# Fourier mixing and a gated feed-forward: batch 1's input in one run, and a transpose cut in four pieces

## The chip, the cores and the metric

The kernel runs on one core of a Trainium2 chip. The metric is the device time of one execution in microseconds (us). The engines are named as in the profile: PE is TensorE, DVE is VectorE, ACT is ScalarE, POOL is GpSimd and SP is SyncE, which only issues transfers.

## What is computed

```python
# x: (8, 3008, 256); filters: (1505, 256) real and imaginary; feed-forward 256 -> 1536 -> 256
X = np.fft.rfft(x, axis=1)
Y = X * (filt_r + 1j * filt_i)[None]
y = np.fft.irfft(Y, n=3008, axis=1).reshape(24064, 256)
out = (np.maximum(y @ w_gate, 0) * (y @ w_val)) @ w_out
```

## The kernel before

A sequence of 3008 = 94 x 32 rows is transformed in two steps, and back in two. Step A is a transform of length 94 by matmul, step B one of length 32, then the filter's product, then the two inverse steps. The order of all instructions is written out by hand: each engine does its own in the order of the program, and semaphores hold it until its inputs are there and its outputs may be overwritten.

Batches 0 and 1 take step A from x in fp32, loaded into XF0 and XF1 (`load_x`, L185; 16 columns of 256 each, 96 partitions in three transfers). `first_a(b, p, s, h, copy)` (L278) is one sixteenth of step A for batch b: `p` picks a quarter of the 32 columns (p = 0 and 1 lie in XF0, p = 2 and 3 in XF1), `s` a half of that quarter and `h` one half of the 256 channels. A matmul goes to a bank of PSUM, and ACT copies it as bf16 into the tile `AS[b][h]`. `turn_a(b, h)` (L288) then transposes one half, 128 x 2048 as fp32 words, in blocks of 32 x 32 on DVE into `at`, which step B reads.

`first_b` (L419) is step B, the product and the first inverse step of batch 0, in six groups `i`: `fwd` (PE, into psX), `product` (DVE, or ACT and POOL, into tt and uu), and `inv` (L389: PE into psD, a copy to `dsb`, and every one or two groups a store to `Dbuf` in device memory, L416). The store that ends with group 3 is issued by ACT, the others by SP. After each group `amid(i)` puts in other work: spare matmuls (`warm`), the rest of batch 1's x after group 3, half of the gate and value weights after group 5 (`load_vg`, POOL), and one `first_a` of batch 1 after each of groups 4 and 5 and after the last but one `inv`. The last store of D, two copies wide, comes out of the tile `AS[0][0]`.

`load_d(b, z0, z1, engs)` (L438) reads D back in four chunks `z`, two transfers of 48 partitions each. Chunk 0 of batch 0 is read by SP and ACT, chunk 1 by SP, chunks 2 and 3 by POOL behind the second half of the weights. `hold_gpsimd` makes POOL wait for chunk 0. `item_c(k, h)` (L459) is the last inverse step for block k of 512 rows: PE into psY, and a copy to yT (half 0 by ACT, half 1 by DVE). The 13 `first_a` of batch 1 that are left, and its two `turn_a`, stand around the first `item_c`.

The feed-forward runs over 47 blocks of 12 steps. `gv` (L476) is a step: four matmuls into psV and psG, ACT's copy `vsb`, and DVE's `prod`; `o_part` adds four matmuls for the block before. Other work is bound to a step by `at_step`: clearing of the chunks XP (POOL) at step 2, the other batches' step A on POOL and PE, step B of batch 1 from step 16 on, and `item_c` of the next block at steps 8 and 10 of each block. PSUM's eight banks are taken in turn, so a step can't be more than four steps ahead of its `prod`.

The tiles of the start (XF, AS, tabs, tt, uu, xs) lie in a pool `pro` that is closed ahead of the feed-forward, whose pool `fs` (vsb, prod, XP and others) takes its place. In the program as built, the first `vsb` waits for the transpose of `AS[1][1]`.

Of the kernel before, what the change touches and what calls it, by code (L numbers as in the profile page):

```python
# [12 lines left out]
FP32 = mybir.dt.float32  # L13
BF16 = mybir.dt.bfloat16
# [15 lines left out]
N1, N2 = 94, 32  # L30
NROW = 96
NG = 24
# [3 lines left out]
def _ap(t, offset_elems, ap_list):  # L36
    return dataclasses.replace(
        t, offset=t.offset + offset_elems, ap=[list(p) for p in ap_list]
    )
# [81 lines left out]
def kernel(  # L121
# [10 lines left out]
    nc = tc.nc  # L132
    B, S_, D = x.shape
# [3 lines left out]
    NC2 = 8  # L137
# [11 lines left out]
    sb = ctx.enter_context(tc.tile_pool(name="sb", bufs=2))  # L149
# [3 lines left out]
    def bank(name, *shape):  # L153

        i = free.pop(0)
        t = ps.tile([128, *shape], FP32, tag=f"bank{i}", bufs=1, name=name)
        held[id(t)] = i, t
        return t

    def done(t):  # L160
        free.append(held.pop(id(t))[0])

    prologue = ExitStack()
    pro = prologue.enter_context(tc.tile_pool(name="pro", bufs=1))

    Abuf = [dram.tile([NROW * N2, D], BF16, name=f"Abuf{b}") if b > 1 else None for b in range(B)]
    Dbuf = [dram.tile([NROW * N2, D], BF16, name=f"Dbuf{b}") for b in range(B)]

    XF = [pro.tile([128, NX2 * D], FP32, name=f"XF{c}") for c in range(N2 // NX2)]
    WA = pro.tile([128, 128], FP32)  # L170
    AS = [[pro.tile([128, NC2, N2 // NC2, D // 2], BF16, name=f"AS{b}{h}") for h in range(2)]
          for b in range(2)]
    WF = consts.tile([128, 4, 32], FP32)
    M1 = consts.tile([NROW, N1], BF16)
    F2 = consts.tile([128, NG, 64], BF16)
# [9 lines left out]
    def load_x(b, engs, cols, ms=range(3)):  # L185
        w = NX2 * D
        for c, c0, c1 in cols:
            for m in ms:
                rows = min(32, B * N1 - (b * N1 + 32 * m))
                engs[m % len(engs)].dma_start(XF[c][m:m + 4 * rows - 3:4, c0:c1],  # L190
                              _ap(x, (b * N1 + 32 * m) * N2 * D + c * w + c0,
                                  [[N2 * D, rows], [1, c1 - c0]]))
# [57 lines left out]
    def place_filter(fi, a, half, copy):  # L250

        dst = FILT[fi][1]
        gs = slice(H * half, H * half + H)
        r = a * 64
        copy(dst[r + 32:r + 64, gs, :], dst[r:r + 32, gs, :])

    def place_nyq():
        for (src, dst), n in zip(FILT, nyq):
            nc.gpsimd.tensor_copy(dst[96:97, NG - 1, :], n)

    def load_vg(c0, c1):
        for (w_hbm, w_sb) in ((moe_w_val, WvT), (moe_w_gate, WgT)):
            nc.gpsimd.dma_start(w_sb[:, :, c0:c1],
                                _ap(w_hbm, c0, [[DFF, 128], [128 * DFF, 2], [1, c1 - c0]]))
# [7 lines left out]
    def hold_gpsimd(tile_):  # L272

        scr = sb.tile([128, 8], FP32, tag="scr", bufs=2)
        nc.gpsimd.tensor_copy(scr[:tile_.shape[0]], tile_)  # L275


    def first_a(b, p, s, h, copy):  # L278

        psA = bank("psA", 4, D // 2)  # L280
        xf = XF[p // 2].rearrange("p (n d) -> p n d", d=D)
        n = p % 2 * NC2 + 4 * s
        nc.tensor.matmul(psA, WA, xf[:, n:n + 4, h * D // 2:(h + 1) * D // 2],  # L283
                         start=True, stop=True)
        copy(AS[b][h][:, 4 * s:4 * s + 4, p, :], psA)
        done(psA)

    def turn_a(b, h):  # L288

        if h == 0:  # L290
            ats[b] = sb.tile([128, 32, D], BF16, tag="at", bufs=1, name="at")
        src = AS[b][h].rearrange("p l c d -> p (l c) d").bitcast(FP32).rearrange("p n d -> p d n")
        dst = ats[b].bitcast(FP32).rearrange("p k d -> p d k")
        nc.vector.transpose(dst[:, h * D // 4:(h + 1) * D // 4, :], src)  # L294

    fold = {}

# [91 lines left out]
    def inv(b, i, cuts=CUTS):  # L389

        if i in cuts:
            if (b, i) == (0, 5):
                dsb = AS[0][0].rearrange("p (a o) c d -> p a (o c d)", a=2)
                dsb = dsb.rearrange("p a (o d) -> p a o d", d=D)
            else:
                dsb = sb.tile([128, 2, 4, D], BF16, tag="dsb", bufs=3, name="dsb")
            dsbs[b] = i, dsb
        i0, dsb = dsbs[b]
        psD = [bank("psD", 2, D) for a in range(2)]
        for m in range(2):  # L400
            for k in range(2):
                for a in range(2):
                    for e in range(2):
                        nc.tensor.matmul(psD[a][64 * e:64 * e + 64, m],  # L404
                                         (I2t, I2u)[k][64 * a:64 * a + 64, 4 * i + 2 * m + e, :],
                                         tus[b, i, e, k][64 * a:64 * a + 64, m],
                                         start=(k == 0), stop=(k == 1),
                                         tile_position=(64 * a, 64 * e))
        o = 2 * (i - i0)
        for a in range(2):  # L410
            copy = nc.vector.tensor_copy if (b, i, a) == (0, 5, 0) else nc.scalar.copy
            copy(dsb[:, a, o:o + 2, :], psD[a])  # L412
            done(psD[a])
        if i + 1 in cuts:
            eng = nc.scalar if (b, i) == (0, 3) else nc.sync
            eng.dma_start(_ap(Dbuf[b], 2 * i0 * D, [[NG * D, 128], [NG // 2 * D, 2], [1, (o + 2) * D]]),  # L416
                              dsb[:, :, :o + 2, :])

    def first_b(amid):  # L419
# [18 lines left out]
    def load_d(b, z0=0, z1=NZ, engs=(nc.sync, nc.sync)):  # L438
        for z in range(z0, z1):
            dC = sb.tile([NROW, 8, D], BF16, tag="dC", bufs=6)  # L440
            for e in range(2):
                engs[e].dma_start(dC[48 * e:48 * e + 48],
                                  _ap(Dbuf[b], (64 * e + 16 * z) * NG * D,
                                      [[D, 48], [48 * D, 8], [1, D]]))
            dCs[b, z] = dC
# [87 lines left out]
    def warm(n, cols=512):  # L533

        psJ = bank("psJ", 512)
        for i in range(n):
            nc.tensor.matmul(psJ[:, :cols], junk[:, 0:128], junk[:, :cols], start=True, stop=True)
        done(psJ)

    q = NX2 * D // 4  # L540
    both, sp = (nc.sync, nc.scalar), (nc.sync,)
# [19 lines left out]

    warm(18, 256)
    for p, s, h in [(p, s, h) for p in range(2) for s in range(2) for h in range(2)]:
        first_a(0, p, s, h, nc.scalar.copy)
    for p, h in ((2, 0), (3, 0), (2, 1), (3, 1)):
        for s in range(2):
            first_a(0, p, s, h, nc.scalar.copy)
    for i in range(3):
        make_back_t(i)
    for i in range(3):  # L570
# [1 line left out]
    for h in range(2):  # L572
        turn_a(0, h)
# [3 lines left out]
    place_filter(1, 0, 0, nc.gpsimd.tensor_copy)  # L577
    for fi, a, half in ((0, 0, 0), (0, 1, 0), (1, 1, 0), (0, 0, 1), (0, 1, 1), (1, 0, 1), (1, 1, 1)):
        place_filter(fi, a, half, nc.sync.dma_start)
    load_x(1, sp, ((0, 0, 2 * q),))  # L580
    early = iter([(p, s, h) for h in range(2) for p in range(4) for s in range(2)])

    def amid(i):
        if i == 3:
            place_nyq()
            load_x(1, sp, ((0, 2 * q, 4 * q), (1, 0, 4 * q)))
        if i == 5:
            load_vg(0, DFF // 2)
        if i < 4:
            warm(3)  # L590
        for _ in range((0, 0, 0, 0, 1, 1, 1)[i]):
            first_a(1, *next(early), nc.scalar.copy)

    first_b(amid)
    load_d(0, 0, 1, (nc.sync, nc.scalar))
    load_d(0, 1, 2)
    hold_gpsimd(dCs[0, 0][:, 7, D - 8:])
    load_vg(DFF // 2, DFF)
    load_o()
    load_d(0, 2, 4, (nc.gpsimd, nc.gpsimd))  # L600
    for i, (p, s, h) in enumerate(early):
        first_a(1, p, s, h, nc.scalar.copy)
        if (p, s, h) == (3, 1, 0):
            turn_a(1, 0)
        if i == 9:
            for hc in range(2):
                item_c(0, hc)
    turn_a(1, 1)
    nc.sync.dma_start(WF, nc.inline_tensor(fold_h, name="dft_fold").ap())
    prologue.close()  # L610
    fs = ctx.enter_context(tc.tile_pool(name="fs", bufs=2))
# [9 lines left out]
    def at_step(s, f):  # L621
        side.setdefault(s, []).append(f)

    C_AT = (8, 10)
    at_step(2, clear_chunks)
    for b in range(1, B):
        end = (b * S // W - 1) * NFT + C_AT[0] - 5
        if b > 1:
            for j, e in enumerate((-74, -69, -62, -55) if b == 2 else (-74, -69, -64, -57)):
                l = (22, 29, 34, 43)[j] if b == 2 else end - 115 + NFT * j  # L630
# [11 lines left out]
        for i in range(7):  # L642
            l = -35 + 5 * i if b == 1 else -40 + 6 * i
# [8 lines left out]
    for k in range(NB):  # L652
        prods = []
        for ft in range(NFT):
# [3 lines left out]
            for f in side.get(k * NFT + ft, ()):  # L658
                f()
            if ft in C_AT and k + 1 < NB:  # L660
                item_c(k + 1, C_AT.index(ft))
        prev = (k, prods)
# [30 lines left out]
```

## Time and profile before

| | us |
|---|---|
| median of three runs (lowest, highest) | 894.89 (893.23, 897.41) |
| the profiled execution | 893.3 |
| its span, first to last instruction | 891.5 |

| engine | busy us | share of the span | instructions |
|---|---|---|---|
| PE | 873.1 | 98% | 7193 |
| DVE | 573.7 | 64% | 860 |
| ACT | 499.0 | 56% | 897 |
| POOL | 373.4 | 42% | 373 |

The page cuts the span into 40 slices of 22.3 us and gives each engine's busy share in tenths. The chain of waits is followed back from the last instruction: each piece is what the next one waited for. A line of the timeline or of the chain begins with the start and the length in us; in square brackets stands how long the engine sat idle before it, and what ended that. A line of a window has, for each engine, the busy time and the number of instructions, then PE's granted clock, the mean busy share of the 16 DMA engines and the GB/s that they moved. A line of the waits gives the total, the number of times and the longest, in us.

### The profile page before, as it was taken

How to read it: one execution, taken by the hardware profiler on the slowest of the kernel's cores; microseconds unless marked ns; L12 is line 12 of the kernel's file. 1: busy time of each engine (PE TensorE's matmuls, PEld its weight loads, DVE VectorE, ACT ScalarE, POOL GpSimd, SP SyncE). 2: the span in 40 equal slices, each digit the busy share in tenths (PEclk: the TensorE clock that was granted, in tenths of full speed). 3: DMA queues.
4: the chain of work that ended last, by engine and by line, in shares of the span. 5: the costliest groups of instructions: out<-in, count | busy, mean ns of one | idle time of the engine just before them, and what ended most of it. 6: DMA issues, size and time to landing. Idle time of an engine off the chain costs nothing.

```text
span 891.5 us, 19155 instructions
## 1 busy us (share of the span) xinstructions
PE 873.1 (98%) x7193; PEld 508.7 (57%) x7193; DVE 573.7 (64%) x860; ACT 499.0 (56%) x897; POOL 373.4 (42%) x373
## 2 busy tenths in 40 slices
PE   9779999999999999999999999999999999999998
PEld 4335555556556665566655566556655556666665
DVE  3657865577665776667766677657766577655553
ACT  5545565556555556555655565555565555655553
POOL 7531698038661486416672167802868000000001
PEclk9999999999999999999999999999999999999999
DMA  9892548534366335463375434763446512331111
GB/s 249 243 179 40 137 128 169 126 96 124 114 159 136 117 95 145 130 140 93 100 175 132 99 100 113 180 134 79 115 136 155 119 32 83 81 75 36 37 30 55
DMA packets 105587, 104.41 MB, mean 117 GB/s; under 512 B 20167, under 2 KB 90343, under 8 KB 104918
## 3 DMA queue, kind: packets, MB, share of 16 engines
q1 hardware_dynamic: 81606, 74.75, 33.1%
q0 software_dynamic: 22864, 27.19, 13.1%
q8 instruction: 57, 0.93, 0.5%
q10 hardware_dynamic: 1024, 1.25, 0.4%
q14 instruction: 36, 0.29, 0.1%
HBM read 58.93 MB, written 46.66 MB: 118 GB/s over the span
## 4 chain that ended last, share of the span: by engine, by line
PE 89%; DMA 5%; DVE 2%; SPq 1%; issue 1%; ACT 1%; POOL 0%; ACTq 0%; DVEq 0%; POOLq 0%
PE psV L481 27%; PE psO L502 26%; PE psG L481 26%; PE psF L330 3%; PE psY L465 2%; PE psD L404 2%; DMA dC<-Dbuf 2%; PE psX L367 2%; PE psA L283 1%; DVE at L294 1%; DMA XF<-in_x_dram 1%; DMA at<-Abuf 1%; DMA Dbuf<-AS 1%; SPq L348 1%; SPq L190 1%
## 5 line engine op out<-in xcount | busy, mean ns | idle before, releaser
L486 DVE SCALAR_TENSOR_TENSOR prod<-psG,vsb 128x512 bf16<-128x512 f32 x564 | 388.5, 690 | 259.4 <-ACT vsb L484 254.5
L484 ACT CAST vsb<-psV 128x512 bf16<-128x512 f32 x564 | 331.5, 589 | 265.5 <-PE psV L481 175.3
L481 PE MATMUL psV<-yT,WvT 128*128 128x512 bf16 x1128 | 336.8, 379 | 2.7 <-ACT vsb L484 1.7
L502 PE MATMUL psO<-WoT,prod 128*128 128x256 bf16 x2256 | 336.4, 273 | 0.0
L481 PE MATMUL psG<-yT,WgT 128*128 128x512 bf16 x1128 | 335.3, 379 | 0.1
L502 PEld LDWEIGHTS <-prod 128*128 128x128 bf16 x2256 | 220.7, 98 | 143.4
L481 PEld LDWEIGHTS <-WgT 128*128 128x128 bf16 x1128 | 110.0, 98 | 135.4 <-issue 2.6
L481 PEld LDWEIGHTS <-WvT 128*128 128x128 bf16 x1128 | 98.4, 98 | 42.4 <-issue 31.3
L275 POOL CAST scr<-prod 128x8 f32<-128x8 bf16 x24 | 4.5, 189 | 252.6 <-DVE prod L486 252.6
L526 POOL DMA_DIRECT2D out_dram<-osb x5 | 2.6, 535 | 195.7 <-ACT osb L515 195.7
L515 ACT COPY osb<-psO 128x512 f32<-128x512 f32 x92 | 53.9, 586 | 25.9 <-PE psO L502 25.2
L316 POOL TENSOR_TENSOR fold<-XP 128x1024 f32<-128x1024 f32 x24 | 56.5, 2356 | 21.6 <-PE psF L330 19.2
L383 DVE TENSOR_TENSOR tt<-psX,Ftr 128x512 bf16<-128x512 f32 x96 | 64.9, 681 | 1.0 <-ACT xs L380 0.3
L383 DVE TENSOR_TENSOR uu<-psX,Fti 128x512 bf16<-128x512 f32 x88 | 59.9, 681 | 0.0
L303 POOL DMA_DIRECT2D XP<-in_x_dram x96 | 56.5, 593 | 2.8 <-PE psY L465 1.4
L317 POOL TENSOR_TENSOR XP<-XP 128x1024 f32<-128x1024 f32 x24 | 56.4, 2349 | 1.9
L412 ACT CAST dsb<-psD 128x512 bf16<-128x512 f32 x94 | 50.6, 591 | 11.0 <-PE psD L404 11.0
L337 ACT CAST asb<-psF 128x512 bf16<-128x512 f32 x48 | 25.8, 589 | 30.5 <-PE psF L330 30.5
L337 DVE CAST asb<-psF 128x512 bf16<-128x512 f32 x48 | 30.9, 686 | 18.3 <-PE psF L330 17.6
L470 ACT CAST yT<-psY 128x512 bf16<-128x512 f32 x47 | 27.7, 588 | 23.9 <-PE psY L465 23.7
L465 PE MATMUL psY<-M,dC 96*128 96x94 bf16 (+18 forms) x604 | 37.7, 198 | 2.0 <-DMA dC<-Dbuf 2.0
L465 PEld LDWEIGHTS <-dC 96*128 96x128 bf16 x604 | 34.4, 97 | 6.4 <-issue 2.3
(70 smaller groups left out, 505.3 us busy)
## 6 DMA issues: line engine op xcount, KB each, us to landing
XP<-in_x_dram POOLq DMA_DIRECT2D x48, 256.0 KB, 6.2
dC<-Dbuf SPq DMA_DIRECT2D x59, 192.0 KB
Dbuf<-dsb SPq DMA_DIRECT2D x22, 512.0 KB
XP<-in_x_dram POOLq DMA_DIRECT2D x96, 96.0 KB, 2.7
Abuf<-asb SPq DMA_DIRECT2D x96, 96.0 KB
at<-Abuf SPq DMA_DIRECT2D x24, 384.0 KB
out_dram<-osb SPq DMA_DIRECT2D x69, 94.0 KB
XF<-in_x_dram SPq DMA_DIRECT2D x15, 256.0 KB
```

Of the source, the lines that this page charges most:

```text
L303: nc.gpsimd.dma_start(xp[r:r + 24, 0:4:2, :], _ap(x, (b * N1 * N2 + o) * D, [[N2 * D, 24], [47 * N2 * D, 2], [1, 512]]))
L316: tt(t, xp[:, 0:2], xp[:, 2:4], op=ALU.add)
L317: tt(xp[:, 2:4], xp[:, 0:2], xp[:, 2:4], op=ALU.subtract)
L337: copy(asf[:, :, q, :], banks[q])
L383: nc.vector.tensor_tensor(p, psX, filt, op=ALU.mult)
L412: copy(dsb[:, a, o:o + 2, :], psD[a])
L465: nc.tensor.matmul(psY[:, o:o + w], dCs[b, n2 // 8][:, n2 % 8, h * 128:(h + 1) * 128], M1[:, n1:n1 + w], start=True, stop=True)
L481: nc.tensor.matmul(pt[:, :W], w[:, h, ft * 128:(ft + 1) * 128], yt[:, h, :], start=(h == 0), stop=(h == 1))
L484: nc.scalar.copy(vsb, psV[:, :W])
L486: nc.vector.scalar_tensor_tensor(prod, in0=psG[:, :W], scalar=0.0, in1=vsb, op0=ALU.max, op1=ALU.mult)
L502: nc.tensor.matmul(psO[:, t % 2], prods[ft][:, t * 128:(t + 1) * 128], WoT[:, ft, :], start=(ft == 0), stop=(ft == NFT - 1))
L515: copy(osb[:, t0 % 2:t % 2 + 1], psO[:, t0 % 2:t % 2 + 1])
```

## The change

Four things change. The nine transfers of batch 1's x are issued in one run by SP, behind the copies of the filters and ahead of all stores of D; before, six of them stood behind the first store. The store that ACT issued, and the half of chunk 0 that ACT read, are SP's. The order of batch 1's `first_a` is new: the four of p = 0 (both halves of the channels) come first, then p = 1 to 3 of half 0, then of half 1. And half 1 of batch 1 no longer goes to an AS tile of its own in `pro`, but to two tiles of 128 x 2048 bf16 from the pool `sb` (those of tag `asb` that later batches use), by two ACT copies of half the width for each `first_a`; it is transposed in four pieces of 128 x 512 words, one behind each of the feed-forward's steps 1, 3, 5 and 7, where before the whole half was transposed ahead of step 0.

```diff
-    AS = [[pro.tile([128, NC2, N2 // NC2, D // 2], BF16, name=f"AS{b}{h}") for h in range(2)]
-          for b in range(2)]
+    AS = [[pro.tile([128, NC2, N2 // NC2, D // 2], BF16, name=f"AS{b}{h}")] for b, h in ((0, 0), (0, 1), (1, 0))]
...
-    def first_a(b, p, s, h, copy):
+    def first_a(b, p, s, h):
...
-        copy(AS[b][h][:, 4 * s:4 * s + 4, p, :], psA)
+        if len(AS) == 3 and (b, h) == (1, 1):
+            AS.append([sb.tile([128, NC2 * D], BF16, tag="asb", bufs=3, name="asb").rearrange(
+                "p (l c d) -> p l c d", l=NC2, c=N2 // NC2) for _ in range(2)])
+        w = D // 2 // len(AS[2 * b + h])
+        for i, t in enumerate(AS[2 * b + h]):
+            nc.scalar.copy(t[:, 4 * s:4 * s + 4, p, :], psA[:, :, i * w:(i + 1) * w])
         done(psA)
...
-    def turn_a(b, h):
+    def turn_a(b, h, i=0, d0=0, d1=None):
...
-        src = AS[b][h].rearrange("p l c d -> p (l c) d").bitcast(FP32).rearrange("p n d -> p d n")
+        src = AS[2 * b + h][i].rearrange("p l c d -> p (l c) d").bitcast(FP32).rearrange("p n d -> p d n")
+        w = src.shape[1]
+        d1 = d1 or w
         dst = ats[b].bitcast(FP32).rearrange("p k d -> p d k")
-        nc.vector.transpose(dst[:, h * D // 4:(h + 1) * D // 4, :], src)
+        o = h * D // 4 + i * w
+        nc.vector.transpose(dst[:, o + d0:o + d1, :], src[:, d0:d1, :])
...
         if i + 1 in cuts:
-            eng = nc.scalar if (b, i) == (0, 3) else nc.sync
-            eng.dma_start(_ap(Dbuf[b], 2 * i0 * D, [[NG * D, 128], [NG // 2 * D, 2], [1, (o + 2) * D]]),
+            nc.sync.dma_start(_ap(Dbuf[b], 2 * i0 * D, [[NG * D, 128], [NG // 2 * D, 2], [1, (o + 2) * D]]),
...
-    load_x(1, sp, ((0, 0, 2 * q),))
-    early = iter([(p, s, h) for h in range(2) for p in range(4) for s in range(2)])
+    load_x(1, sp, ((0, 0, 2 * q), (0, 2 * q, 4 * q), (1, 0, 4 * q)))
+    early = iter([(0, s, h) for h in range(2) for s in range(2)] +
+                 [(p, s, h) for h in range(2) for p in range(1, 4) for s in range(2)])
...
             place_nyq()
-            load_x(1, sp, ((0, 2 * q, 4 * q), (1, 0, 4 * q)))
...
-    load_d(0, 0, 1, (nc.sync, nc.scalar))
-    load_d(0, 1, 2)
+    load_d(0, 0, 2)
...
-    turn_a(1, 1)
...
+    for k in range(4):
+        at_step(1 + 2 * k, lambda k=k: turn_a(1, 1, k // 2, k % 2 * 16, k % 2 * 16 + 16))
```

## The prediction

> **What bounds the kernel now.** I read the page first. TensorE (PE) is 98% busy and the chain that ended last is 89% PE, so the long feed-forward is paced by matmuls, and an edit can only pay in the 11% that the chain spends elsewhere, most of it at the start.
>
> ```profile
> span 891.5 us, 19155 instructions
> ...
> DMA  9892548534366335463375434763446512331111
> ...
> PE 89%; DMA 5%; DVE 2%; SPq 1%; issue 1%; ACT 1%; POOL 0%; ACTq 0%; DVEq 0%; POOLq 0%
> ```
>
> The chain in order of time, between 28 and 75 us, shows these parts (start, us, what):
>
> ```profile
> 35.45 4.64 DMA XF<-in_x_dram
> ...
> 40.18 1.85 PE psA L283 x2
> ...
> 43.82 7.47 DMA Dbuf<-AS
> 51.45 4.09 DMA dC<-Dbuf
> ...
> 55.67 0.62 PE psY L465 x12
> 56.29 2.68 PE psA L283 x6
> 59.00 0.59 ACT AS L285
> 59.62 4.25 DVE at L294
> 64.00 0.59 ACT vsb L484
> ```
>
> So the start is a line: x for batch 1, the last store of D for batch 0, the first read of D, the first yT, and then the second transpose of batch 1, for which the first copy of the feed-forward (vsb, ScalarE) waits. PE has 8.4 us of holes between 36.8 and 65 us. Next, the table of windows over the stretch that ends with the last store (after the clock: mean DMA share and GB/s):
>
> ```profile
> 27.00:32.00 5.00, 4.39 (x69) 1.90 (x66) 4.72 (x8) 3.68 (x8) 4.85 (x5) 1.00 0.77 218
> 32.00:34.40 2.40, 2.02 (x30) 0.89 (x34) 2.33 (x4) 2.40 (x6) 2.34 (x4) 1.00 0.06 20
> 34.40:40.50 6.10, 2.73 (x44) 1.49 (x44) 2.04 (x4) 3.66 (x8) 3.99 (x5) 0.99 0.96 286
> 40.50:44.00 3.50, 3.50 (x20) 1.04 (x18) 0.69 (x1) 1.17 (x2) 0.00 (x0) 0.53 1.08 405
> 44.00:51.20 7.20, 5.67 (x14) 2.39 (x13) 0.00 (x0) 0.00 (x0) 0.00 (x0) 1.00 0.91 212
> ```
>
> From 34.4 to 51.2 us the DMA engines are full, so the last store is late because of bytes, not because of its issue. Ahead of that stretch they stand empty for 2.4 us. SP's waits and timeline say why: a store of D, waiting for ScalarE, stood ahead of the rest of batch 1's x.
>
> ```profile
> SPq L416 <- ACT xs L380: 4.5, 1, 4.5
> ```
>
> ```profile
> 33.04 0.61 SPq L416 DMA_DIRECT2D Dbuf<-dsb  x1
> 33.76 4.29 SPq L190 DMA_DIRECT2D XF<-in_x_dram  x6
> ```
>
> Last, VectorE (DVE) after the first yT:
>
> ```profile
> 59.62 4.23 DVE L294 STREAM_TRANSPOSE at<-AS 128x2048 f32<-128x2048 f32 x1
> 64.62 5.71 DVE L486 SCALAR_TENSOR_TENSOR prod<-psG,vsb 128x512 bf16<-128x512 f32 x9 [0.77 <-ACT vsb L484]
> 70.78 1.50 DVE L486 SCALAR_TENSOR_TENSOR prod<-psG,vsb 128x512 bf16<-128x512 f32 x2 [0.46 <-ACT vsb L484]
> 72.20 0.68 DVE L472 CAST yT<-psY 128x512 bf16<-128x512 f32 x1
> ```
>
> It is nearly gapless from 59.62 to 72.88 us, and the second block's first matmul on its yT half begins at 72.94. Feed-forward block 0 is therefore bound by VectorE, and moving a transpose inside it saves only gaps.
>
> **The change, part by part.** *x in one run.* Nine transfers are issued back to back from 27.15 us: three took 1.83 us and six 4.29, so SP is through at 33.3. The first store of D waits for ScalarE until 33.04 anyway, so passing it costs 0.3 us of issue. What moves is bytes: the store now lies behind all of x in one queue, and the hole is filled. Work from 27 to 51.2 us, share times length: 3.85 + 0.14 + 5.86 + 3.78 + 6.55 = 20.2 us of full engines. The full stretch averages 16.2 / 16.8 = 0.96, so without a hole the same work ends at 27 + 20.2 / 0.96 = 48.0 us instead of 51.2. That is the last store if it ends together with the first half of the weights (GpSimd's queue, issued at 37.0, first packet at 42.5 in the packet records; between 45 and 50 us the two queues send packets one for one). If weights again start late, the stores run out sooner: at most by the weights' 4.3 us of engine time, 43.5. Bounds 43.5 and 50; I take 47.8, near the first, since a drained queue lets the weights in earlier. **Minus 3.4 us.**
>
> *The order of batch 1's first steps.* The third A step now reads p = 0, landed before 33 us, so PE does not wait for x until 40.18. Then 36.8 + 0.86 (one A step) + 0.7 (inverse) + about 1.2 of copies: the last store is issued near 39.6 instead of 43.82. It lies behind the backlog in either case, so this is worth nothing by itself; without it the store would be the limit again at 43.8 + 2.
>
> *Stores and reads of D from SP alone.* ScalarE loses two issues (0.61 and 0.38 us) and, more, its wait: the page's groups have it standing 8.5 us before 52.2, with PE's A steps held by full banks. After, the ten A steps end at 38.4 + 10 x 0.86 = 47.0, and batch 1's first transpose (4.2 us) lies in the shadow too. SP's four reads are issued one after another: the second half of chunk 0 0.46 us later than now, but ahead of chunk 1 in the same queue instead of beside it. Bounds for the read, 4.2 us now: 3.4 to 4.7. I take 3.8, **minus 0.4**. The Trainium skill, "DMA: Bandwidth & Descriptors", section "Rules for kernel authors", says that spreading transfers over issuing engines saves issue time alone; by that the move would cost 0.46, and the sum would be 0.9 us worse. No run here shows it yet.
>
> *The transpose in four pieces.* Each is a quarter of 4.23 us, 1.06. The second half's copies become two of 128x256: 0.29 apart in the I2t row (1.76 us for six), 0.45 at the longest, against 0.59 for one; six lie behind the first yT, where PE takes 2.6 us for its three A steps, so they hide, bar 0.3 us. Now from the first read's landing T: 12 yT matmuls and three A steps put the first gate matmul at T + 3.2 and the first vsb's end at T + 4.65 (ScalarE's last A copies end at T + 4.06). VectorE then does eleven products at 0.634, four pieces and one yT copy: 6.97 + 4.24 + 0.68 = 11.9, ending at T + 16.6. Before it was 72.88 - 55.64 = T + 17.2. **Minus 0.6**; bounds minus 1.2 (no gaps, vsb at T + 4.1) and plus 0.6 (each piece with 0.3 us around it). PE's stall of 2 us at 62.4 goes, but the products are what is late next. GpSimd's chunk clearing now lies beside the pieces.
>
> *PE's clock.* From 47.0 to T (51.7) PE has nothing. Before, the idle stretch from 36.8 to 40.2 was followed by a clock of 0.53 (the row of 40.5). Half clock for 3.4 us costs 1.7, of which ScalarE's A copies hide some: bounds 0 and 1.9, and I take 0.7, since it depends on how the stretch falls. **Plus 0.7.** The Trainium skill, "TensorE: Matmul & The Clock Gate", section "HAM oscillation — how this bites in real kernels", allows no PE-idle gap over about 3.4 us; it speaks against this change, and taken as certain it would price the step at 1.7 and the sum at minus 2.7.
>
> Later weights, D reads and x loads hang on T or on products and shift along. The weights' second half lands at 62.8, T + 7.2, and its first user comes at T + 8.8.
>
> **Sum:** -3.4 - 0.4 - 0.6 + 0.7 = -3.7. Against the profiled execution's 893.3 (span 891.5 and 1.8 around it): 889.6. The runs' median, 894.89, lies 1.6 above that execution, which is the fast end of the three; I take half of it: 890.4.
>
> **Rivals.** *The weights stay late* (for it: 42.5, 5 us after their issue; against: the queue ahead of them is emptier after 39 us). The last store lands near 44.3, T near 48.2, PE idles 1.2 us and keeps its clock: -7.0 - 0.4 - 0.6 = -8.0, or 886.
>
> *The run is no run*: SP waits inside it, each transfer also for the landing of the one eight places before, so x arrives as now, and only the gapless block and the earlier store stay: about -1, 893. Against it: the transfers eight before are filter copies issued by 27 us, gone by 29.
>
> *VectorE's pieces beside GpSimd's memsets* end on the other side. The four memsets (7.04 us from 63.96 now) would run from T + 6 to T + 13, just beside the pieces. If the two hinder each other, each piece is longer; at 1.06 + 0.93 = 2.0 us a piece the whole gain is gone, at 3.0 us it is 4 x 1.94 - 3.7 = +4.1, or 898. Against it: the transposes at 17.4 us took 4.17 to 4.26 with a GpSimd copy of 2.73 us in their midst.
>
> **How the numbers follow.** Forecast 0.62 (its own range 888.3 to 892.6), late weights 0.18, no run 0.13, hindered pieces 0.07. The 8-in-10 range reaches into the neighbours on both sides: 886.8 to 893.6. 0.5%, about what a measurement of this kernel can tell from no change, is 4.5 us, so the line is 890.4, the forecast's middle: faster 0.31 + 0.17 = 0.48; slower 0.06, nearly all from the hindered pieces; the rest, 0.46, is same.
>
> **What would show it.** Right: DMA share above 0.9 from 28 to 48 us with no hole at 32; the last store landing at 47 to 48.5; the first dC wait ending at 50.5 to 52.5; no vsb wait on a transpose; pieces of 1.0 to 1.1 us; yT's second half at T + 16 to 17. A clock of 0.5 after T shows the 0.7 too small. Wrong: stores landing past 50, pieces over 1.5 us, or a gate matmul waiting for weights.

## The result, and the profile after

The changed kernel took 891.91 us (median of 20 runs, 890.25 to 895.38) where the kernel before took 895.35 (20 runs, 893.23 to 899.71). The ratio is 0.9963 with a 95% interval of 0.9952 to 0.9974: the medians differ by 3.4 us, under the line of 0.5% (4.5 us). The forecast was 890.4 within 886.8 to 893.6. The profiled execution took 891.76 us, near its median; the one of before lies 2 us below its own median, so the two profiles show 1.5 us of the 3.4.

From the page after:

```profile
span 890.0 us, 19171 instructions
...
DMA  9991448534366336553375334762446512331111
...
PE 91%; DMA 4%; DVE 2%; issue 1%; POOL 1%; SPq 1%; ACT 0%; DVEq 0%; POOLq 0%; ACTq 0%
```

The same windows, as far as 54 us, show where time was won and where it was lost again (the three columns at the end are clock, DMA share and GB/s; PE's busy time is the first after the length):

```profile
32.00:34.40 2.40, 2.01 (x28) 0.98 (x27) 2.06 (x4) 2.40 (x6) 2.40 (x3) 1.00 1.00 307
34.40:40.50 6.10, 6.10 (x66) 2.75 (x65) 3.31 (x6) 5.67 (x14) 4.53 (x7) 1.00 0.94 321
...
48.00:51.20 3.20, 0.00 (x0) 0.00 (x0) 2.16 (x1) 0.54 (x2) 0.00 (x0) 0.96 0.16 47
51.20:54.00 2.80, 0.35 (x5) 0.36 (x6) 0.00 (x0) 0.00 (x0) 0.30 (x2) 0.50 1.19 223
```

The hole at 32 us is full, and PE works through to 47.9 us. Then it stands for 5.8 us, and when the read of D comes its clock is at half (the 0.96 in the row of 48.00 is a fall at 50.9 us; the half clock lasted until 57.8). The chain shows both, and what the half clock costs:

```profile
39.80 9.62 DMA Dbuf<-AS
49.56 0.33 SPq L448
...
49.95 3.65 DMA dC<-Dbuf
...
53.65 1.03 PE psY L471 x12
54.68 4.26 PE psA L282 x6
```

Before, the same two steps of PE took 0.62 and 2.68 us; here 1.03 and 4.26. The first matmul of the feed-forward (into psV; the expectations call it the gate matmul) starts at 58.8 us, as it did before, though the read ended 1.9 us sooner. VectorE's lines show the pieces and the yT behind them, and GpSimd's line the memsets beside them:

```profile
61.49 1.20 DVE L301 STREAM_TRANSPOSE at<-asb 128x512 f32<-128x512 f32 x1
...
68.28 1.21 DVE L301 STREAM_TRANSPOSE at<-asb 128x512 f32<-128x512 f32 x1
69.39 1.86 DVE L492 SCALAR_TENSOR_TENSOR prod<-psG,vsb 128x512 bf16<-128x512 f32 x3
71.15 0.69 DVE L478 CAST yT<-psY 128x512 bf16<-128x512 f32 x1
```

```profile
59.44 7.09 POOL L621 MEMSET XP<- 128x2048 f32 x4
```

The piece at 61.49 lies beside the memsets, the one at 68.28 behind them, and they last 1.20 and 1.21 us.

### The profile page after: what moved, and what is told of

Read it like the earlier page. It is cut to its first block, busy times and chain, and to the rows that moved or that the text cites. A ratio compares the mean times of both kernels' runs of the same rounds, so it can differ in the third digit from the quotient of the medians.

```text
span 890.0 us, 19171 instructions
## 1 busy us (share of the span) xinstructions
PE 873.0 (98%) x7193; PEld 509.5 (57%) x7193; DVE 573.7 (64%) x863; ACT 501.2 (56%) x905; POOL 374.0 (42%) x373
## 4 chain that ended last, share of the span: by engine, by line
PE 91%; DMA 4%; DVE 2%; issue 1%; POOL 1%; SPq 1%; ACT 0%; DVEq 0%; POOLq 0%; ACTq 0%
PE psV L487 28%; PE psG L487 27%; PE psO L508 26%; PE psF L337 3%; PE psY L471 2%; PE psD L411 2%; DMA dC<-Dbuf 2%; PE psX L374 2%; PE psA L282 2%; DMA Dbuf<-AS 1%; DVE at L301 1%; DMA XF<-in_x_dram 1%; DVE prod L492 0%; SPq L189 0%; DMA Dbuf<-dsb 0%
## 5 line engine op out<-in xcount | busy, mean ns | idle before, releaser
L419 ACT CAST dsb<-psD 128x512 bf16<-128x512 f32 x94 | 50.6, 592 | 10.9 <-PE psD L411 10.9
```

## The experiments

Two readings of the small gain stood against each other. The clock theory: the earlier read is worth 2 us or more, and PE's idle stretch turns most of it into a half clock. The VectorE theory: block 0 is paced by VectorE, and nothing that PE does there counts. Of the bytes, the packet-turn theory said that the last store is late because its packets take turns with those of the weights.

**The changed kernel again**, as the measure for the runs beside it.

> The changed kernel once more, as the measure for the other runs of this call. Every theory: 0.995 to 0.997 of the kernel before. Clock theory (the changed kernel loses most of what it wins because TensorE idles about 5.8 us ahead of the first read of D and then runs at half clock for 3.4 to 7 us): a half-clock stretch shows again after the first read, of other length, and the first gate matmul comes 4.5 to 5.2 us after the read where it lasts, 3.2 where it does not. VectorE theory (block 0 is bound by VectorE whatever the clock does): the second block's first yT half ends 16.5 to 18.5 us after the read in either case.

891.59 us, 0.9949 (0.9930 to 0.9967). That is 4.9 us under the kernel before, where the first comparison gave 3.4. The clock was 0.5 again from 50.6 us on, for 6.8 us, and the gate matmul came 5.0 us after the read's end.

**Spare matmuls in the gap.**

```diff
         if i == 9:
+            warm(20)
             for hc in range(2):
```

> The changed kernel with 20 spare matmuls of 512 columns (0.216 us each, 4.3 us) on TensorE between its tenth A step of batch 1 and the wait for the first read of D. Clock theory: the granted clock stays 1.0 after the read, the first gate matmul comes 3.2 us after it instead of 5.1, and the time falls by 1.2 to 2.0 us against the changed kernel (0.994 to 0.995 of the kernel before). VectorE theory: the gate matmuls start earlier but the second block's yT ends no earlier, and the time stays within 0.4 us of the changed kernel's.

889.0 us, 0.9916 (0.9894 to 0.9938): 2.6 us under the changed kernel on the same chip. Twice more, on other chips: 889.45 us, 0.9937 (0.9920 to 0.9955), and 889.73 us, 0.9938 (0.9914 to 0.9961). By their ratios to the kernel before, these two lie 1.0 to 2.3 us under the two measurements of the changed kernel.

> The changed kernel with 20 spare matmuls between TensorE's tenth A step and the wait for the first read of D, once more, as the measure for the other runs of this call. Clock theory: 0.991 to 0.993 of the kernel before, clock 1.0 after the read, the gate matmul 3.2 us and the yT of block 1 about 16.3 us after it.

> The changed kernel with 20 spare matmuls, on the same chip as the run with later weights: 0.991 to 0.994 of the kernel before, 889 to 889.5 us, with the clock at 1.0 throughout.

The clock stayed at 1.0 in all three profiles. PE's timeline in the first of them, and a row of its windows:

```profile
47.80 4.48 PE L543 MATMUL psJ<-junk 128*128 128x512 bf16 x20
52.11 0.63 PE L471 MATMUL psY<-M,dC 96*128 96x94 bf16 x12
52.59 2.82 PE L282 MATMUL psA<-XF,WA 128*128 128x512 f32 x6
55.24 0.59 PE L487 MATMUL psV<-yT,WvT 128*128 128x512 bf16 x2
...
53.00:56.00 3.00, 3.00 (x10) 1.25 (x9) 0.47 (x1) 1.98 (x8) 3.00 (x6) 1.00 0.88 103
```

The gate matmul follows the first yT matmul by 3.1 us, and VectorE's yT for block 1 ends 16.2 us after the read (18.2 with the half clock). In the third profile the read ended at 53.7 us, as in the changed kernel's (53.6), and this yT 1.9 us sooner. The changed kernel's own executions point the same way: of its first 20, the five with a mean clock of 0.998 took 890.25 to 891.35 us (median 890.5), the fifteen with 0.995 or 0.996 took 891.14 to 895.38 (median 892.5); of the six runs here the one with 0.998 took 893.0. The clock theory holds; the VectorE theory, in the form that the clock does not count, falls. This version is faster than both kernels.

**The transpose whole**, ahead of the first step, once with the half clock and once with the spare matmuls.

```diff
+    for k in range(2):
+        turn_a(1, 1, k)
     nc.sync.dma_start(WF, nc.inline_tensor(fold_h, name="dft_fold").ap())
...
-    for k in range(4):
-        at_step(1 + 2 * k, lambda k=k: turn_a(1, 1, k // 2, k % 2 * 16, k % 2 * 16 + 16))
```

> The changed kernel with the second half of batch 1 turned in two pieces of 128x1024 words back to back ahead of the feed-forward's first step, instead of in four pieces behind steps 1, 3, 5 and 7; the two asb tiles stay, so the first vsb has no wait on the transpose. If the four places matter: TensorE stalls again for 1 to 2 us after four steps, and the yT of block 1 ends 0.5 to 1 us later. VectorE theory (the same 4.2 us of transposes and eleven products in either order): the yT of block 1 ends within 0.5 us of where it did, and the time is within 0.6 us of the changed kernel's.

> The kernel with the 20 spare matmuls, and the second half of batch 1 turned whole (two pieces of 128x1024 words) ahead of the first step. VectorE theory, with the clock out of the way: eleven products, 4.3 us of transposes and a yT copy in a row either way, so the yT of block 1 ends within 0.6 us of where it does with four pieces, and the time differs by less than 1 us. If the places of the pieces carry the gain: 1 to 2.5 us slower than with four pieces.

892.0 us, 0.9955 (0.9941 to 0.9969), against 891.59 in four pieces; with the spare matmuls 889.16 us, 0.9933 (0.9913 to 0.9952), against 889.45. VectorE's lines in the second, where the read ended at 54.5:

```profile
58.24 4.33 DVE L301 STREAM_TRANSPOSE at<-asb 128x1024 f32<-128x1024 f32 x2 [2.38 <-ACT asb L289]
62.47 5.67 DVE L492 SCALAR_TENSOR_TENSOR prod<-psG,vsb 128x512 bf16<-128x512 f32 x9
68.59 1.50 DVE L492 SCALAR_TENSOR_TENSOR prod<-psG,vsb 128x512 bf16<-128x512 f32 x2 [0.46 <-ACT vsb L490]
70.01 0.68 DVE L478 CAST yT<-psY 128x512 bf16<-128x512 f32 x1
```

The yT ends 16.2 us after the read here too. PE waits 1.5 us for a product in the middle of the block, as expected, and less at its end. Here the VectorE theory is right: the order of its work within the block is worth nothing that can be measured.

**One part alone, on the kernel before.** First the x in one run:

```diff
-    load_x(1, sp, ((0, 0, 2 * q),))
+    load_x(1, sp, ((0, 0, 2 * q), (0, 2 * q, 4 * q), (1, 0, 4 * q)))
...
             place_nyq()
-            load_x(1, sp, ((0, 2 * q, 4 * q), (1, 0, 4 * q)))
```

> The kernel before with one edit: batch 1's x in one run. Byte theory (the empty 2.4 us of the DMA engines are what is won): the last store lands 1.5 to 3 us earlier than before's 51.3 and the time falls by 1 to 3 us; TensorE's A steps stay held by full banks while ScalarE waits for its read, so it works until about 2 us before the read and keeps its clock. Rival (the store's own issue, and ScalarE's wait, set it): no change within 0.7 us.

892.05 us, 0.9968 (0.9954 to 0.9982): about 3 us, of 3.4 and 4.9 that the whole change gave in its two measurements. The last store landed at 49.4 us, as with the whole change. The expected clock was a miss in the profile: with x early, PE came to the full banks earlier too, stood for 4.65 us, and its clock fell. The mean clocks of the twelve executions run from 0.995 to 1.0, so it did not fall in every one.

```profile
50.93 3.78 PE L283 MATMUL psA<-XF,WA 128*128 128x512 f32 x4 [4.65 <-ACT AS L285]
54.51 1.06 PE L465 MATMUL psY<-M,dC 96*128 96x94 bf16 x12
```

Then the pieces alone: the edits to AS, `first_a` and `turn_a` and the four `at_step`, with loads, queues and order as before.

> The kernel before with one edit: the second half of batch 1's A goes to two asb tiles and is turned in four pieces during the first steps. The prediction's sum: the yT of block 1 ends 0.6 us sooner counted from the first read of D, and the time falls by 0.3 to 1.2 us. If the wait of the first vsb on the transpose was worth its 4.4 us: 2 to 4 us faster.

894.48 us, 0.9995 (0.9980 to 1.0011): no change that can be measured, and the interval leaves out the 2 to 4 us. The yT of block 1 ended 16.8 us after the read instead of 17.2. The 4.4 us that the first vsb had waited for the transpose were not lost time, since the products had to follow the transpose on VectorE either way.

**ScalarE's two transfers given back** to it, in the changed kernel:

```diff
-            nc.sync.dma_start(_ap(Dbuf[b], ...
+            eng = nc.scalar if (b, i) == (0, 3) else nc.sync
+            eng.dma_start(_ap(Dbuf[b], ...
...
-    load_d(0, 0, 2)
+    load_d(0, 0, 1, (nc.sync, nc.scalar))
+    load_d(0, 1, 2)
```

> The changed kernel with ScalarE's two transfers given back: the second store of D and the second half of chunk 0's read. The prediction's step (SP alone is worth 0.4 us in the read): the read takes 4.2 us from issue instead of 3.8 to 4.1, and the time is 0.3 to 1 us above the changed kernel's (0.996 to 0.998 of the kernel before). Rival, the clock: ScalarE waits for the last store ahead of its read and holds TensorE's A steps by full banks, so that some of them fall behind the wait; they are then in the way of the first yT, at half clock, and the time is 1 us or more above the changed kernel's. If the two transfers do not matter: within 0.3 us.

892.55 us, 0.9966 (0.9948 to 0.9984). The read took 4.3 us from its issue, against 4.0 in the changed kernel's profile, and two A steps fell behind ScalarE's wait and ran at half clock; but the half clock lasted 3.41 us and ended at 54.8 us, 2.9 us sooner than in the changed kernel's profile. By the ratios the time lies 0.3 us above the first measurement of the changed kernel and 1.5 above the second, with intervals that overlap both, so this run can't tell what the queues are worth.

**The weights later.** `load_vg(0, DFF // 2)` and GpSimd's work behind it move into the loop of the later A steps, behind a wait for the fourth of the loop's copies (the expectation counts it as the fifth):

```diff
-        if i == 5:
-            load_vg(0, DFF // 2)
...
         first_a(1, p, s, h)
+        if i == 3:
+            hold_gpsimd(AS[2][0][:, 0, 2, 0:8])
+            load_vg(0, DFF // 2)
+            ...     # hold on chunk 0, second half of the weights, load_o, chunks 2 and 3
```

> The changed kernel with the first half of the gate and value weights issued by GpSimd only when the fifth of the later A steps of batch 1 has been copied (about 43.4 us instead of 37.8), so that they leave the DMA engines to the last three stores of D. Packet-turn theory (the stores are late because each of their packets takes turns with one of the weights): the last store lands at 44.5 to 46 instead of 49.5, the first read at 48.5 to 50 instead of 53.6, TensorE idles 1 to 2 us and keeps its clock, and the time falls by 4 to 6.5 us against the changed kernel (about 0.990 of the kernel before). Rival, that the stores are bound by their own 1 KB pieces: the last store lands no earlier than 48, and the time moves by less than 1.5 us. If the weights become the limit, the first gate matmul waits for them.

892.02 us, 0.9953 (0.9934 to 0.9971): no gain, and yet the store did what packet turns foretold. Its landing moved from 49.4 to 44.9 us, and the read behind it took 7.5 us. The chain:

```profile
39.91 5.04 DMA Dbuf<-AS
...
45.48 7.53 DMA dC<-Dbuf
```

The weights had been issued from 43.67 us on, ahead of the read at 45.10; the read's first packet came at 49.0, when seven tenths of the weights' packets were through. The theory priced the store rightly and left out that the read then has the weights in front of it.

**Later still**, behind the sixth copy (`if i == 5`, `AS[2][0][:, 0, 3, 0:8]`), and behind the eighth (`if i == 7`, `AS[3][0][:, 0, 1, 0:8]`; the expectations say seventh and ninth) with `warm(8)` ahead of the first yT:

> The kernel with the first half of the weights issued late, 2.5 us later still: GpSimd waits for the seventh of the later A steps' copies (about 46 us), so that the weights come behind the first read of D instead of ahead of it. Packet-turn theory: the last store lands near 45 as with the weights at 43.4, but the read takes 3 to 4.2 us instead of 7.5, its end is near 48.5 to 49.5, TensorE idles under 2 us and keeps its clock, the first gate matmul starts at 51.7 to 53 (limited by the weights' landing near 50 to 52.5), and the time falls to 884.5 to 887.5 us (0.988 to 0.991 of the kernel before). Rival, that a read of D costs about 7 us whenever weights follow it: no better than the changed kernel.

> The changed kernel with the first half of the weights issued at about 47.2 us (behind the ninth of the later A steps' copies, so behind the issue of the first read of D by 1.5 us or more) and 8 spare matmuls (1.7 us) on TensorE ahead of the first yT. Packet-turn theory: the last store lands near 45, the read takes 3 to 4.2 us undisturbed and ends at 48.5 to 50, the clock stays at 1.0, the first gate matmul pair is limited by the weights' landing near 52.5 to 54, and the time is 885.5 to 888.5 us, below the kernel with 20 spare matmuls alone (889). If the weights' landing costs what the read wins: within 1 us of that kernel.

The first took 890.77 us, 0.9944 (0.9923 to 0.9964): the sixth copy ended at 45.1 us, where the 46 that I had reckoned with is the end of the seventh, the weights were again issued just ahead of the read, at 45.35 against 45.46, and the read took 5.8 us. The second, 890.68 us, 0.9948 (0.9927 to 0.9968), is a miss that teaches most. The store landed at 46.5, the read took 3.8 us, the clock held at this point, and the first yT matmul started at 50.5 us, 5 us sooner than in the kernel before. Then the first two pairs of matmuls of the feed-forward waited for the weights, 0.4 and 1.3 us, and between 76 us and the end PE waited for these:

```profile
PE psY L471 <- DMA dC<-Dbuf: 2.1, 1, 2.1
PE psX L374 <- DMA at<-Abuf: 1.9, 1, 1.9
```

That is batch 1's first read of D, near 139 us, and the read of batch 2's step A, near 182. In the first of these waits the clock fell once more, from 140.9 to 144.4 us. In the kernel before they cost 1.15 and 0.2 us, in the first run with 20 spare matmuls 1.55 and 0.55, in its third none. The last product of block 0 started 4.0 us ahead of the kernel before in this run and the last product of all 0.3 us behind it: the lead won at the start was given back where a transfer does not move along with PE. This profile is of the slowest of the eight executions, 2.9 us above their median, so these waits are at the upper end; the two executions with a mean clock of 1.0 took 889.05 and 890.01 us.

## Why the prediction was right or wrong

The time lay inside the range and the sign was right; the middle was 1.5 us too low. Of this, 1.3 is the base: the sum started from 894.1, and the kernel before had a median of 895.35 over 20 runs. That the medians then differ by 3.4 us, close to the sum's 3.7, is partly luck, since the two profiles differ by 1.5 and the terms counted in them give 1.8. The profile of before is one of its executions with a high clock: 0.997 on average, where the 75 executions of this kernel beside the experiments average 0.9945 and only seven reach 0.997; the changed kernel's 20 average 0.996, like its profile. So in most executions the kernel before seems to lose more clock than its profile shows, and the change to win some of that back; where, no trace here shows. Point by point:

- *The hole.* The step held: full engines from 32 us, with nine transfers issued in 5.66 us. The last store landed at 49.4 us, where 47.8 was taken; x itself started 0.9 us later in this execution, 28.02 instead of 27.15, behind the filters' copies. Counted from x, the store came 2.7 us sooner, not 3.4. The weights' first packet came at 41.6 us, 4.0 us after their issue (before it was 42.2 on the time axis of the views, 5.2 after the issue), and their last packet within 0.6 us of the store's, so the weights and the store did end together, as the 48.0 of the sum assumes, and the late weights of the rival were not to be seen. The part alone shows this step as the carrier of the gain.
- *The read.* 3.8 us was taken, 4.0 measured in the profile, against 4.2 before. Over the seven profiles with the read from SP alone and the weights' place unchanged it took 3.7 to 4.2 us, over the four with both queues 4.0 to 4.3, so some 0.3 of the 0.4 came on average. The rule of the Trainium skill, "DMA: Bandwidth & Descriptors", section "Rules for kernel authors", is that spreading over queues saves issue time alone; the 0.46 us that the move should cost by it is not to be seen, and giving the queue back saved none.
- *The pieces.* 1.06 us a piece was an underestimate: 1.20 each, 1.10 from one start to the next instruction's. Cut or whole made no difference; with the clock up, yT ended 16.2 us after the read with either, 1.0 us better than before, where 0.6 was taken. So the cut itself is not what won this; the pieces alone, on the kernel before, gave 0.4. The rest probably comes from batch 1's first transpose, which ended ahead of the read instead of standing before the first yT copy; that is argued, not shown.
- *The clock.* This is the term that was mis-sized. 0.7 was taken, for a chance of one stretch of 3.4 us; the clock fell in all seven profiles of kernels with x in one run and without spare matmuls, and lasted 6.8 us in five of them, 3.4 in two. The spare matmuls price it at 2.6 us in time on one chip, 1.0 to 2.3 by the ratios of the two other runs, and at 2.0 in the trace (yT at 18.2 against 16.2 after the read). With 2.0 in place of 0.7, 2.7 and 0.1 for the store and the read, and 1.0 for the block, the sum is -2.7 - 0.1 - 1.0 + 2.0 = -1.8 for these two profiles, which differ by 1.5. The rule of the Trainium skill, "TensorE: Matmul & The Clock Gate", section "HAM oscillation — how this bites in real kernels", which allows no idle gap over about 3.4 us and was set against the change, should have been taken as certain: the gap cost the clock in both profiles of this kernel (5.8 and 5.6 us).
- *Hindered pieces* did not happen: 1.20 us beside the memsets, 1.21 behind them. *The run is no run* did not either.
- What the prediction did not have at all: later transfers that do not shift with T. It said that D reads and x loads hang on T or on products; batch 1's D read and batch 2's `at` cost between nothing and 4 us over these runs, and that is a part of why single profiles differ.

## What to carry to other kernels

Filling an empty stretch of the DMA engines ahead of a full one was worth about its length here (2.4 us empty, the last store 2.7 us sooner), and reordering inside the full stretch mostly moved the wait to the next transfer in line (the store 4.5 us sooner, the read behind it 3.5 us longer). When a wait is shortened by letting an engine run ahead of it, that engine idles in one long stretch where it idled in several short ones: look at what clock it comes back with, and fill the stretch with spare matmuls if need be. A lead won at the start has to be followed to the end, past every transfer that has its own time.

## What the runs showed of the hardware

- In all 14 traces every stretch of one clock, from its first rise to the last microseconds, is a whole multiple of 3.41 us long (34.1, 37.5, 44.4 or 47.8 us ahead of the first fall near the start; the half clock 3.41 or 6.83). Cut at these points, PE's busy time in one piece of 3.41 us goes with the clock of the next. Of the pieces at full clock, the ten with at most 1.28 us of work were all followed by half clock, and none of the 3589 with 1.49 us or more was. Of the pieces at half clock, the five with at most 2.52 us were followed by another, the ten with 2.96 us or more by full clock. The nearest rows on either side, in this order, are of the runs with the weights behind the eighth copy, of the pieces alone (kept its clock), of the weights behind the fourth copy (stayed at half) and of the pieces alone (came back):

```profile
137.53:140.94 3.41, 1.28 (x11) 0.72 (x9) 0.37 (x1) 0.96 (x2) 1.26 (x1) 1.00 1.17 171
...
45.24:48.65 3.41, 1.49 (x4) 0.80 (x5) 0.00 (x0) 0.00 (x0) 0.00 (x0) 1.00 1.08 245
...
52.16:55.58 3.42, 2.52 (x14) 1.69 (x15) 0.69 (x1) 0.59 (x1) 2.47 (x5) 0.50 0.95 114
...
41.83:45.24 3.41, 2.96 (x18) 0.96 (x18) 0.69 (x1) 1.17 (x2) 0.00 (x0) 0.50 1.03 366
```

  As an estimate from these numbers, an idle gap of more than 4.3 us between stretches of full work costs the clock wherever it falls, and one under 1.9 us never does. In the changed kernel the two pieces from 47.5 us on held 0.35 and 0.69 us of work, and 6.83 us at half clock came of it.
- So a fall of the clock can come while PE is working: at 40.38 us in the kernel before, 0.20 us after its return from 3.4 us of idling, and 0.8 us after its return with the weights behind the sixth copy.
- A read of 192 KB issued 1.4 us behind 768 KB of weights on another queue had its first packet 3.9 us after its issue, against 1.0 us with the engines empty (the changed kernel). Stores and weights, both in flight, had sent packets nearly one for one from 45 to 49 us in the kernel before; this read, new to engines busy with the weights, did not get such turns at first.
